# Attention features and FFN on one core: q and k transposed by VectorE in blocks of 32, v loaded in the matching token order

## The chip, the cores and the metric

One core of a Trainium2 chip runs the whole program. The metric is the device time of one execution in microseconds; several runs are made and their median is compared. Beside the timed runs there is one profiled execution, from which all durations of single instructions come.

## The reference

Polysketch attention, followed by a feed-forward network with a squared ReLU. All inputs and the output are fp32. There are 4 batches, 4 heads, 1088 tokens and a head width of 32; the FFN has width 128 and inner width 2048.

```python
def phi(x):                                   # features: 8 x 8 = 64 per token and head
    a = np.einsum('rd,bhsd->bhsr', S1, x)
    b = np.einsum('rd,bhsd->bhsr', S2, x)
    return np.einsum('bhsi,bhsj->bhsij', a, b).reshape(*x.shape[:-1], r * r)
q_p, k_p = (phi(q), phi(k))
kv = np.einsum('bhsf,bhsd->bhfd', k_p, v)     # summed over all tokens of a batch
z = np.sum(k_p, axis=2)
num = np.einsum('bhsf,bhfd->bhsd', q_p, kv)
den = np.einsum('bhsf,bhf->bhs', q_p, z)[..., None] + 1e-06
attn = (num / den)                            # then heads side by side: x is [4352, 128]
h = np.maximum(x @ w_in, 0.0)
out = h * h @ w_out
```

## The kernel before

**Tokens.** Of the 1088 tokens of a batch, 1024 are "main" tokens, eight consecutive ones on each of 128 partitions (token 8p + j on partition p). They are treated in two groups g of four, j = 4g to 4g + 3, so a group has 512 tokens: 4 tiles of 128 tokens. The last 64 tokens of each batch, the remainder, are treated by pairs of batches. A group of 512 tokens is a chunk for the FFN; with the remainder of all batches there are nine chunks, the eighth main one last.

**Features.** `load` fetches a batch of q, k or v as one transfer of 512 KB into a tile of the pool "inp" (two buffers for each of q, k and v). `proj_t` turns a group: for each head TensorE transposes 128x128 (partition p against j and head dimension) into PSUM (`xt_ps`, L194), and ScalarE copies it to `xt` (L59, the line of the helper `evict`; four buffers). `proj` multiplies `xt` with `w_bd`, a block-diagonal matrix of S1 and S2 (L180, `ab_ps`), ScalarE copies that out (`ab`), and POOL, in the start VectorE, makes the outer products (L221, `ph`). For k, `Kv` sums `ph` against v and a column of ones (L249, `kv_ps`), and VectorE copies the result to `kvbd`. For q, `feature_t` transposes `ph` by TensorE (L299, `t_ps`), `numerators` multiplies with `kvbd` (L180, `nd`), `normalize` divides on VectorE (L329 to L358, `xs`) and turns the quotient by TensorE (L370), which is `xT`, a chunk's input for the FFN.

**v.** The tile of `load` has 32 columns per head and token; `spread_v` copies it, one copy per head on POOL, to `v_main`, where each head has 33 columns, the last one of ones. `v_main` exists twice, for even and odd batches. `spread_vrem` does the same for the remainder. In the start, batch 0, ScalarE and POOL share the copies.

**FFN.** A chunk takes 16 blocks. In a block TensorE makes a `pg` (fp16, L534), ScalarE its ReLU (`gt`, L537), VectorE the square (`g2`, which the profile calls g, L538), and TensorE adds the product with `w_o` (fp32, L554, for the last chunk L563) to `po`. `first_product` runs two blocks ahead (`LOOK`). A finished chunk is copied and transposed back (L493, L497), scaled by VectorE (L511, `o_sb`, two buffers) and stored by SP (L519).

**Order.** `start()` is laid down by hand: batch 0's k, and q of its first group, down to the first `xT`; the second group's q is begun there (`second`). After it a scheduler orders the instructions of each engine; some, marked `pinned`, keep the program's order. The main loop runs over batches: two stretches of 16 blocks, between which `pump` emits steps of the waiting generators (`k_gen` of the next batch and `q_gen` of this one in the first stretch, `q_gen` of the next batch in the second). `drain` empties them. After the first stretch of batch b the loads of batch b + 2 are issued. All loads but four small ones and all stores are issued by SP, in one queue; each issue waits on one of eight semaphores, so that a transfer starts only when the one eight places before it has landed.

Of the kernel before, what the change touches and what calls it, by code (L numbers as in the profile page):

```python
# [8 lines left out]
F32 = mybir.dt.float32  # L9
# [12 lines left out]
def kernel(  # L22
# [39 lines left out]
    def pinned(ins):  # L62

        tc.keep_in_program_order(ins)
# [18 lines left out]
    def load(src, b, tag, pin=False):  # L83
        t = inpool.tile([128, H * NJ * D], F32, tag=tag)
        ins = load_part(t, src, b, 0, NJ)
        if pin:
            pinned(ins)
        return t

    def load_rem(src, r, eng, tag):  # L90
        t = inpool.tile([128, E], F32, tag=tag)
        for u in range(2):
            eng.dma_start(
                _v(t, 0, [[D, H], [1, D]], 64 * u, 64), rows(src, 2 * r + u, SM, 64, 1, 1)
            )
        return t

    s_nat = cpool.tile([16, E], F32)
    for i, src in enumerate((S1, S2)):
# [1 line left out]
            _v(s_nat, 0, [[D, H], [1, D]], 8 * i, 8),  # L101
            bass.AP(src.tensor, src.offset, [[D, 8], [0, H], [1, D]]),
        )
    k_sb, q_sb, v_sb, k_rm, q_rm, v_rm = {}, {}, {}, {}, {}, {}
    for x, tag in ((k_sb, "k_sb"), (q_sb, "q_sb"), (v_sb, "v_sb")):
        x[0] = inpool.tile([128, H * NJ * D], F32, name=f"{tag}0", tag=tag)
    load_part(k_sb[0], k, 0, 0, 4)
# [2 lines left out]
    load_part(q_sb[0], q, 0, 0, 4)  # L110
    load_part(v_sb[0], v, 0, 0, 4)
    load_part(v_sb[0], v, 0, 4, 4)
    v_rm[0] = load_rem(v, 0, nc.sync, "v_rm")
    w_in32 = cpool.tile([128, DFF], F32)
    for c in range(2):
        nc.sync.dma_start(
# [6 lines left out]
        bass.AP(moe_w_out.tensor, moe_w_out.offset, [[E, 128], [128 * E, NC], [1, E]]),  # L123
    )
    k_sb[1] = load(k, 1, "k_sb")
    v_sb[1] = load(v, 1, "v_sb")
    q_rm[0] = load_rem(q, 0, nc.sync, "q_rm")
    q_sb[1] = load(q, 1, "q_sb")


# [7 lines left out]
    w_bd = cpool.tile([128, H * 16], F32)  # L138
    nc.vector.memset(w_bd[:], 0.0)
    kvbd = [cpool.tile([128, 4 * VW], F32, name=f"kvbd{i}") for i in range(2)]  # L140
    v_main = [cpool.tile([128, NJ * H * VW], F32, name=f"v_main{i}") for i in range(2)]
    v_rem = [cpool.tile([128, H * VW], F32, name=f"v_rem{i}") for i in range(2)]
    iden16 = cpool.tile([128, 128], F16)
    nc.vector.tensor_copy(iden16[:], iden[:])
    for i in range(2):
        nc.vector.memset(kvbd[i][:], 0.0)
        nc.vector.memset(_v(v_rem[i], D, [[VW, H]]), 1.0)
        nc.vector.memset(_v(v_main[i], D, [[VW, H * NJ]]), 1.0)

    def idle_products(n):  # L150
        idle_ps = pspool.tile([128, 512], F32, name="idle_ps", tag="po", bufs=2)
# [6 lines left out]
    def spread_v(b, eng, j0=0, w=NJ, heads=range(H), pin=False):  # L158

        for h in heads:  # L160
# [4 lines left out]
            )  # L165
            if pin:
                pinned(ins)

    def spread_vrem(r, eng, pin=False):
        ins = eng.tensor_copy(  # L170
            out=_v(v_rem[r], 0, [[VW, H], [1, D]]), in_=_v(v_rm[r], 0, [[D, H], [1, D]])
        )
        if pin:
            pinned(ins)

    def tiled(out_ps, c0, w, lhsT, l0, rhs, n=128, p0=0, m=32):

# [9 lines left out]
    def proj_t(src, g, T, eng, tag="ms"):  # L187


        n = 4 if T == 4 else 1  # L190
        w = NJ * D if T == 4 else E
        xt_ps = pspool.tile([128, 512], F32, tag=tag, bufs=2)
        for i in range(n):
            nc.tensor.transpose(  # L194
                xt_ps[:, 128 * i : 128 * i + 128],
                src[:, w * i + 128 * g : w * i + 128 * g + 128],
                iden[:, :],
            )
        xt = apool.tile([128, 512], F32, tag="xt", bufs=4)
        evict(eng, xt[:, 0 : 128 * n], xt_ps[:, 0 : 128 * n])  # L200
        return xt

    def proj(xt, T, tag, eng, outer, ps_tag="ms", m=32):
# [68 lines left out]

    def k_gen(b, outer):
        eng = nc.scalar
        spread_v(b, nc.gpsimd, pin=True)
        if b % 2 == 0:
            spread_vrem(b // 2, nc.gpsimd, True)
        xt = []
        for g in range(2):
            xt.append(proj_t(k_sb[b], g, 4, eng))  # L280
            yield 1
        phs = []
        for g in range(2):
            phs.append(proj(xt[g], 4, "ph_k", eng, outer))
            yield 2
        if b % 2 == 0:
            yield from krem_gen(b // 2, eng, outer)
        kv = Kv(b)
        for g in range(2):
            kv.tiles(phs[g], g, range(4))  # L290
            yield 1
        kv.finish((nc.vector, nc.vector))
        yield 1
# [80 lines left out]
        return beta  # L374

    chunks = []

    def chunk_of(b, g, xT, beta):
        dst = bass.AP(out.tensor, out.offset + (b * S + 4 * g) * E, [[NJ * E, 128], [1, 512]])
        chunks.append((xT, 4, [(beta, 4)], [(dst, 0, 128, 0, 512)]))  # L380

    def x_gen(b, g, phT, m=32):
        nd = numerators(b, phT, m)
# [5 lines left out]

    def q_gen(b, g, outer, m=32):  # L390
        eng = nc.scalar
        xt = proj_t(q_sb[b], g, 4, eng)
        yield 1
        ph = proj(xt, 4, "ph_q", eng, outer, m=m)
        yield 3
        phT = []
        for pr in range(2):
            phT.append(feature_t(ph, 4, pr, eng))
            yield 1
        yield from x_gen(b, g, phT)  # L400
# [105 lines left out]
    def store(po, betas, dsts):  # L506

        o_sb = fpool.tile([128, 512], F32, tag="o_sb", bufs=2)
        t0 = 0
        for beta, n in betas:  # L510
            nc.vector.tensor_tensor(  # L511
                out=_v(o_sb, 128 * t0, [[128, n], [1, 128]]),
                in0=_v(po, 128 * t0, [[128, n], [1, 128]]),
                in1=_v(beta, 0, [[1, n], [0, 128]]),
                op=mult,
            )
            t0 += n
        for dst, p0, n, c0, w in dsts:
            nc.sync.dma_start(dst, _v(o_sb, c0, [[1, w]], p0, n))  # L519

    LOOK = 2
    LAST = 8
# [63 lines left out]
    def start():  # L586
        s_ps = pspool.tile([128, 16], F32, name="s_ps", tag="po", bufs=2)
        xk = [proj_t(k_sb[0], 0, 4, act)]
        nc.tensor.transpose(s_ps[:, :], s_nat[:, :], iden[0:16, 0:16])
        for h in range(H):  # L590
            nc.vector.tensor_copy(
                out=_v(w_bd, 16 * h, [[1, 16]], 32 * h, 32),
                in_=_v(s_ps, 0, [[1, 16]], 32 * h, 32),
            )
        xk.append(proj_t(k_sb[0], 1, 4, act))
        idle_products(2)
        pk = [proj(x, 4, "ph_k", act, (dve,), "pg", m=64) for x in xk]
        idle_products(1)
        xq = proj_t(q_sb[0], 0, 4, act)
        spread_v(0, act, 0, 4)  # L600
        pq = proj(xq, 4, "ph_q", act, (dve,), "pg", m=64)
        xkr = proj_t(k_rm[0], 0, 1, act)
        spread_v(0, act, 4, 4, (0, 1))
        spread_v(0, pool, 4, 4, (2, 3))
        spread_vrem(0, pool)
        ph_krem[0] = proj(xkr, 1, "ph_kr", act, (dve,), "pg", m=64)
        kv0 = Kv(0, 64, "po", 2)
        kv0.tiles(pk[0], 0, range(4))
        pqT = [feature_t(pq, 4, 0, act)]
        kv0.tiles(pk[1], 1, range(4))  # L610
        pqT.append(feature_t(pq, 4, 1, act))
        kv0.finish((dve, dve))
        first = x_gen(0, 0, pqT, 64)
        next(first)
        for c in range(4):
            act.copy(
                w_in[:, 512 * c : 512 * c + 512], w_in32[:, 512 * c : 512 * c + 512]
            )
# [13 lines left out]
    for b in range(B):  # L632
        add_work(second if b == 0 else q_gen(b, 1, (pool,)))
        if b + 1 < B:
            add_work(k_gen(b + 1, (pool,)))
        if b % 2 == 0:
            add_work(qrem_phi_gen(b // 2, (pool,)), qrem_num_gen(b))
        else:
            add_work(qrem_num_gen(b))
        for c in range(NC):  # L640
            block()
            pump_stores()
            pump(2)
        drain()
        if b + 2 < B:
            k_sb[b + 2] = load(k, b + 2, "k_sb", True)
            v_sb[b + 2] = load(v, b + 2, "v_sb", True)
            q_sb[b + 2] = load(q, b + 2, "q_sb", True)
            if b == 0:
                k_rm[1] = load_rem(k, 1, nc.sync, "k_rm")  # L650
                v_rm[1] = load_rem(v, 1, nc.sync, "v_rm")
                q_rm[1] = load_rem(q, 1, nc.sync, "q_rm")
        if b + 1 < B:
            add_work(q_gen(b + 1, 0, (pool,)))
        for c in range(NC):
            block()
            pump_stores()
            pump(2)
        if b + 1 < B:
            drain()  # L660
# [35 lines left out]
```

## Time and profile before

| | |
|---|---|
| three runs | 219.83, 217.87, 219.4 us; median 219.4 us |
| profiled execution | 217.62 us, span 215.8 us, mean granted TensorE clock 0.997 |
| TensorE matmuls (PE) | 207.4 us busy, 96% |
| VectorE (DVE) | 144.3 us, 67% |
| ScalarE (ACT) | 119.1 us, 55% |
| GpSimd (POOL) | 44.8 us, 21% |
| DMA | 11.35 MB, 13575 packets; above 3 tenths of the 16 DMA engines in 7 of 40 slices: the first five and two near 75 us |

The span is the time from the first to the last instruction of the profiled execution; 1.8 us of its time lie outside. PE is TensorE's matmuls, PEld its weight loads, which run beside matmuls. Matmuls are pipelined: a row's mean duration is longer than the distance between two of them. An fp32 matmul that is no transpose stands as two in the rows (a `po` is "x2"). An idle time is put down to what ended it.

### The profile page before, as it was taken

The page shows a single profiled execution, that of the slowest core. Times are in us where ns is not written, and L with a number is a line of the kernel's source. Part 1 is how long each engine was busy: PE and PEld are TensorE (multiplying, and loading weights), DVE is VectorE, ACT ScalarE, POOL GpSimd, SP SyncE. Part 2 cuts the span into 40 slices and gives each one's busy share as a digit, 9 for nine tenths or more (in the row PEclk, how much of TensorE's full clock was granted, in tenths as well). Part 3 has the DMA queues.
Part 4 walks back from the last instruction along what each step waited for, and adds up shares of the span by engine and source line. Part 5 has one row for each costly group of instructions (what it writes and reads, how often), then busy time and mean ns, then how long its engine had stood idle before and what let it go on. Part 6 is the DMA issues. An engine that isn't in the chain of part 4 may idle for free.

```text
span 215.8 us, 5391 instructions
## 1 busy us (share of the span) xinstructions
PE 207.4 (96%) x2253; PEld 125.4 (58%) x2253; DVE 144.3 (67%) x279; ACT 119.1 (55%) x234; POOL 44.8 (21%) x59
## 2 busy tenths in 40 slices
PE   8889999999999999999999999999999899999992
PEld 7677545445545664655546565455545454669992
DVE  2637696658685799557775567657868777677661
ACT  3655654564566555556466663656465456665550
POOL 1302273004050672004120960013101200000000
PEclk9999999999999999999999999999999999999998
DMA  6999900001000460001000100000000000100001
GB/s 172 270 312 319 267 8 3 2 3 49 3 0 0 131 212 3 3 0 52 2 0 0 52 3 2 3 16 36 2 3 19 30 5 0 49 0 15 12 0 49
DMA packets 13575, 11.35 MB, mean 53 GB/s; under 512 B 3824, under 2 KB 11760, under 8 KB 13552
## 3 DMA queue, kind: packets, MB, share of 16 engines
q1 hardware_dynamic: 12928, 10.95, 17.0%
q8 instruction: 17, 0.28, 0.5%
q10 hardware_dynamic: 624, 0.07, 0.2%
q14 instruction: 6, 0.05, 0.1%
HBM read 8.79 MB, written 2.23 MB: 51 GB/s over the span
## 4 chain that ended last, share of the span: by engine, by line
PE 86%; DVE 6%; ACT 1%; issue 1%; DVEq 0%
PE po L554 46%; PE pg L534 14%; PE po L563 7%; PE nd L180 5%; PE t_ps L299 4%; PE kv_ps L249 3%; PE xt_ps L194 3%; PE ab_ps L180 2%; PE o_ps L497 2%; DVE g L538 1%; DVE xs L358 1%; PE x_ps L370 1%; DVE o_sb L511 1%; DVE small L339 1%; ACT xt L59 1%
## 5 line engine op out<-in xcount | busy, mean ns | idle before, releaser
L538 DVE TENSOR_TENSOR g<-gt 128x512 f32<-128x512 f32 (+1 forms) x144 | 104.8, 737 | 50.5 <-ACT gt L537 48.5
L554 PE MATMUL po<-g,w_o 128*128 128x512 f32 (+1 forms) x256 | 124.1, 570 | 1.1 <-DVE g L538 1.1
L537 ACT ACTIVATE gt<-pg 128x512 f32<-128x512 f32 (+1 forms) x144 | 82.6, 576 | 48.2 <-PE pg L534 47.4
L554 PEld LDWEIGHTS po<-g,w_o 128*128 128x128 f32 x256 | 46.7, 191 | 27.8 <-DVE g L538 9.6
L534 PE MATMUL pg<-xT,w_in 128*128 128x512 f16 x128 | 48.6, 381 | 0.1
L221 POOL TENSOR_TENSOR ph<-ab 128x512 f32<-128x512 f32 (+1 forms) x27 | 32.1, 1213 | 69.7 <-ACT ab L59 69.6
L534 PEld LDWEIGHTS <-w_in 128*128 128x128 f16 x144 | 14.2, 99 | 17.7 <-issue 15.0
L59 ACT COPY sb<-t_ps 128x512 f32<-128x512 f32 (+1 forms) x20 | 10.3, 521 | 12.9 <-PE t_ps L299 12.9
L563 PEld LDWEIGHTS po<-w_o,g 128*128 128x128 f32 x128 | 16.3, 192 | 0.8 <-DVE g L538 0.4
L563 PE MATMUL po<-w_o,g 128*128 128x128 f32 x128 | 16.4, 275 | 0.0
L59 ACT COPY xt<-xt_ps 128x512 f32<-128x512 f32 (+1 forms) x20 | 10.3, 524 | 7.1 <-PE xt_ps L194 7.0
L364 POOL TENSOR_TENSOR beta<-mp 128x4 f32<-128x4 f32 (+1 forms) x10 | 3.1, 319 | 52.3 <-DVE mp L346 44.4
L59 ACT COPY ab<-ab_ps 128x256 f32<-128x256 f32 (+1 forms) x20 | 6.8, 340 | 13.0 <-PE ab_ps L180 12.5
L180 PEld LDWEIGHTS nd<-kvbd,sb 128*32 128x32 f32 (+1 forms) x512 | 8.9, 111 | 7.3 <-issue 3.2
L299 PEld LDWEIGHTS t_ps<-iden,ph 128*128 128x128 f32 x68 | 8.4, 141 | 8.0 <-issue 4.9
L180 PE MATMUL ab_ps<-w_bd,xt 128*32 128x64 f32 (+1 forms) x476 | 11.6, 223 | 1.1 <-ACT xt L59 1.1
L180 PEld LDWEIGHTS ab_ps<-w_bd,xt 128*32 128x32 f32 (+1 forms) x476 | 8.7, 113 | 6.5 <-ACT gt L537 3.0
L180 PE MATMUL nd<-kvbd,sb 128*32 128x66 f32 (+1 forms) x512 | 10.8, 222 | 0.7 <-DVE kvbd L60 0.7
L299 PE MATMUL t_ps<-iden,ph 128*128 128x128 f32 x68 | 10.9, 276 | 0.2 <-DVE ph L221 0.2
L194 PEld LDWEIGHTS xt_ps<-iden,t 128*128 128x128 f32 x52 | 6.4, 141 | 5.2 <-issue 2.8
L194 PE MATMUL xt_ps<-iden,t 128*128 128x128 f32 x52 | 8.3, 276 | 0.1
L249 PEld LDWEIGHTS kv_ps<-v_main,ph 128*32 128x32 f32 (+1 forms) x448 | 5.7, 113 | 2.7 <-issue 0.9
(57 smaller groups left out, 115.6 us busy)
## 6 DMA issues: line engine op xcount, KB each, us to landing
out_dram<-o_sb SPq DMA_DIRECT2D x8, 256.0 KB, 2.0
t<-in_k_dram SPq DMA_DIRECT2D x3, 512.0 KB, 6.5
t<-in_v_dram SPq DMA_DIRECT2D x3, 512.0 KB, 7.5
t<-in_q_dram SPq DMA_DIRECT2D x3, 512.0 KB, 7.3
w_in<-in_moe_w_in_dram SPq DMA_DIRECT2D x2, 512.0 KB, 6.0
k_sb<-in_k_dram SPq DMA_DIRECT2D x2, 256.0 KB, 3.1
q_sb<-in_q_dram SPq DMA_DIRECT2D x2, 256.0 KB, 5.7
v_sb<-in_v_dram SPq DMA_DIRECT2D x2, 256.0 KB, 5.6
```

Of the source, the lines that this page charges most:

```text
L59: return nc.scalar.copy(dst, src)
L180: nc.tensor.matmul(out_ps[p0 + c : p0 + c + m, c0 : c0 + w], lhsT[:, l0 + c : l0 + c + m], rhs,)
L194: nc.tensor.transpose(xt_ps[:, 128 * i : 128 * i + 128], src[:, w * i + 128 * g : w * i + 128 * g + 128], iden[:, :],)
L221: outer[(t0 // 2) % len(outer)].tensor_tensor(out=_v(ph, 256 * t0, [[64, 4 * m], [8, 8], [1, 8]]), in0=_v(ab, 64 * t0, [[16, 4 * m], [1, 8 ...
L249: nc.tensor.matmul(self.ps[c : c + self.m, VW * pr : VW * pr + VW], _v(ph, c0 + 128 * pr + c, [[1, self.m]], p0, n), _v(vt, v0 + VW * (2 * ...
L299: nc.tensor.transpose(t_ps[:, 128 * t : 128 * t + 128], ph[:, 256 * t + 128 * pr : 256 * t + 128 * pr + 128], iden[:, :],)
L497: nc.tensor.transpose(o_ps[:, 128 * t : 128 * t + 128], oT[:, 128 * t : 128 * t + 128], iden[:, :])
L534: nc.tensor.matmul(pg[:, 0:nt], w_in[:, 128 * c : 128 * c + 128], xT[:, 0:nt])
L537: nc.scalar.activation(gt[:, 0:nt], pg[:, 0:nt], Relu)
L538: nc.vector.tensor_tensor(out=g2[:, 0:nt], in0=gt[:, 0:nt], in1=gt[:, 0:nt], op=mult)
L554: nc.tensor.matmul(po[0][:, 0:nt], w_o[:, 128 * c : 128 * c + 128], g2[:, 0:nt], start=(c == 0), stop=(c == NC - 1),)
L563: nc.tensor.matmul(po[0][:, 128 * t : 128 * t + 128], g2[:, 128 * t : 128 * t + 128], w_o[:, 128 * c : 128 * c + 128], start=(c == 0 and t ...
```

## The change

Of the sixteen groups of main tokens of k and q, twelve are no longer transposed by TensorE: `turned` has VectorE transpose the whole 128x512 group at once, each block of 32x32 in itself, straight from the loaded tile to `xt`. Only batch 0's k, the first group of q of batch 0 and the last group of q of batch 3 (`BY_PE`) stay with TensorE. Since the blocks stay in their places, a tile of 128 tokens of a turned group holds other tokens than before: tile a has on partition 32j + p' the token 8(32a + p') + 4g + j. v and the output have to follow. `load_v` loads v of batches 1 to 3 straight into `v_main` in this order, by 32 transfers (2 groups, 4 heads, 4 values of j), each to 32 partitions with four runs of 128 bytes on each; the copies of POOL for these batches go. The remainder of v is loaded straight into `v_rem`. A chunk of a turned group is stored by four transfers of 32 partitions instead of one. In the start q_rm[0] is loaded ahead of v of batch 1, and the constant columns of `v_main` and `v_rem` are written before the first loads.

```diff
+    def load_v(b, pin=False):
+        for g in range(2):
+            for h in range(H):
+                for j in range(4):
+                    ins = nc.sync.dma_start(
+                        _v(
+                            v_main[b % 2], 4 * VW * 4 * g + VW * h,
+                            [[4 * VW, 4], [1, D]], 32 * j, 32,
+                        ),
+                        bass.AP(
+                            v.tensor,
+                            v.offset + ((b * H + h) * S + 4 * g + j) * D,
+                            [[NJ * D, 32], [32 * NJ * D, 4], [1, D]],
+                        ),
+                    )
+                    if pin:
+                        pinned(ins)
...
     k_sb[1] = load(k, 1, "k_sb")
-    v_sb[1] = load(v, 1, "v_sb")
     q_rm[0] = load_rem(q, 0, nc.sync, "q_rm")
+    load_v(1)
     q_sb[1] = load(q, 1, "q_sb")
...
+    def turned(src, g):
+        xt = apool.tile([128, 512], F32, tag="xt", bufs=4)
+        nc.vector.transpose(out=xt[:, :], in_=_v(src, 128 * g, [[NJ * D, 4], [1, 128]]))
+        return xt
...
     def k_gen(b, outer):
         eng = nc.scalar
-        spread_v(b, nc.gpsimd, pin=True)
-        if b % 2 == 0:
-            spread_vrem(b // 2, nc.gpsimd, True)
         xt = []
         for g in range(2):
-            xt.append(proj_t(k_sb[b], g, 4, eng))
+            xt.append(turned(k_sb[b], g))
             yield 1
...
+    BY_PE = ((0, 0), (B - 1, 1))
...
+            dsts = [
+                (
+                    bass.AP(
+                        out.tensor, at + j * E, [[NJ * E, 32], [32 * NJ * E, 4], [1, E]]
+                    ),
+                    32 * j, 32, 0, 512,
+                )
+                for j in range(4)
+            ]
...
-        xt = proj_t(q_sb[b], g, 4, eng)
+        xt = proj_t(q_sb[b], g, 4, eng) if (b, g) in BY_PE else turned(q_sb[b], g)
...
             k_sb[b + 2] = load(k, b + 2, "k_sb", True)
-            v_sb[b + 2] = load(v, b + 2, "v_sb", True)
+            load_v(b + 2, True)
             q_sb[b + 2] = load(q, b + 2, "q_sb", True)
             if b == 0:
                 k_rm[1] = load_rem(k, 1, nc.sync, "k_rm")
-                v_rm[1] = load_rem(v, 1, nc.sync, "v_rm")
+                load_rem(v, 1, nc.sync, "v_rm", v_rem[1], VW)
                 q_rm[1] = load_rem(q, 1, nc.sync, "q_rm")
```

More of the change, by code (lines that the diff above doesn't have):

```diff
@@ L88, in load, with load_rem @@
         return t
-    def load_rem(src, r, eng, tag):
-        t = inpool.tile([128, E], F32, tag=tag)
+    def load_rem(src, r, eng, tag, t=None, w=D):
+        if t is None:
+            t = inpool.tile([128, E], F32, tag=tag)
         for u in range(2):
             eng.dma_start(
-                _v(t, 0, [[D, H], [1, D]], 64 * u, 64), rows(src, 2 * r + u, SM, 64, 1, 1)
+                _v(t, 0, [[w, H], [1, D]], 64 * u, 64), rows(src, 2 * r + u, SM, 64, 1, 1)
             )
         return t
+    def load_v(b, pin=False):
[15 more added lines that the diff above has]
+                        pinned(ins)
     s_nat = cpool.tile([16, E], F32)
@@ L103 @@
         )
-    k_sb, q_sb, v_sb, k_rm, q_rm, v_rm = {}, {}, {}, {}, {}, {}
+    k_sb, q_sb, v_sb, k_rm, q_rm = {}, {}, {}, {}, {}
+    v_main = [cpool.tile([128, NJ * H * VW], F32, name=f"v_main{i}") for i in range(2)]
+    v_rem = [cpool.tile([128, H * VW], F32, name=f"v_rem{i}") for i in range(2)]
+    for i in range(2):
+        nc.vector.memset(_v(v_rem[i], D, [[VW, H]]), 1.0)
+        nc.vector.memset(_v(v_main[i], D, [[VW, H * NJ]]), 1.0)
     for x, tag in ((k_sb, "k_sb"), (q_sb, "q_sb"), (v_sb, "v_sb")):
@@ L112 @@
     load_part(v_sb[0], v, 0, 4, 4)
-    v_rm[0] = load_rem(v, 0, nc.sync, "v_rm")
+    load_rem(v, 0, nc.sync, "v_rm", v_rem[0], VW)
     w_in32 = cpool.tile([128, DFF], F32)
@@ L140 @@
     kvbd = [cpool.tile([128, 4 * VW], F32, name=f"kvbd{i}") for i in range(2)]
-    v_main = [cpool.tile([128, NJ * H * VW], F32, name=f"v_main{i}") for i in range(2)]
-    v_rem = [cpool.tile([128, H * VW], F32, name=f"v_rem{i}") for i in range(2)]
     iden16 = cpool.tile([128, 128], F16)
@@ L146 @@
         nc.vector.memset(kvbd[i][:], 0.0)
-        nc.vector.memset(_v(v_rem[i], D, [[VW, H]]), 1.0)
-        nc.vector.memset(_v(v_main[i], D, [[VW, H * NJ]]), 1.0)
     def idle_products(n):
@@ L167, in spread_v @@
                 pinned(ins)
[L169 to L174, printed above, removed]
     def tiled(out_ps, c0, w, lhsT, l0, rhs, n=128, p0=0, m=32):
@@ L376 @@
     chunks = []
+    BY_PE = ((0, 0), (B - 1, 1))
     def chunk_of(b, g, xT, beta):
-        dst = bass.AP(out.tensor, out.offset + (b * S + 4 * g) * E, [[NJ * E, 128], [1, 512]])
-        chunks.append((xT, 4, [(beta, 4)], [(dst, 0, 128, 0, 512)]))
+        at = out.offset + (b * S + 4 * g) * E
+        if (b, g) in BY_PE:
+            dsts = [(bass.AP(out.tensor, at, [[NJ * E, 128], [1, 512]]), 0, 128, 0, 512)]
+        else:
+            dsts = [
[7 more added lines that the diff above has]
+            ]
+        chunks.append((xT, 4, [(beta, 4)], dsts))
     def x_gen(b, g, phT, m=32):
@@ L518, in store @@
         for dst, p0, n, c0, w in dsts:
-            nc.sync.dma_start(dst, _v(o_sb, c0, [[1, w]], p0, n))
+            nc.sync.dma_start(dst, _v(o_sb, c0, [[E, w // E], [1, E]] if n == 32 else [[1, w]], p0, n))
     LOOK = 2
@@ L604, in start @@
         spread_v(0, pool, 4, 4, (2, 3))
-        spread_vrem(0, pool)
         ph_krem[0] = proj(xkr, 1, "ph_kr", act, (dve,), "pg", m=64)
```

## The prediction

> **What bounds the kernel now.** I read the page's first rows, then the chain of waits, then the timelines of PE, VectorE and SP where the change touches them. The busy row and the chain say that TensorE sets the time:
>
> ```profile
> PE 207.4 (96%) x2253; PEld 125.4 (58%) x2253; DVE 144.3 (67%) x279; ACT 119.1 (55%) x234; POOL 44.8 (21%) x59
> ```
>
> ```profile
> 46.48 0.86 PE po L554 x2
> 47.34 0.44 PE xt_ps L194 x4
> 47.99 0.86 PE po L554 x2
> ...
> 72.58 0.45 PE xt_ps L194 x4
> 73.05 0.59 ACT xt L59
> 74.44 0.86 PE po L554 x2
> ```
>
> In the chain (start, length, what) one FFN block is 0.22 us of pg (L534) and 0.86 us of po (L554), 1.08 us; blocks follow each other without a hole, and every other matmul group is inserted between two blocks at its full length. Four transposes of q or k (L194) take 0.44 us. At 73.05 TensorE also waits 0.6 us for the copy of such a transpose by ScalarE; the same is at 120.10. VectorE and ScalarE have idle time on average.
>
> The loads go through one queue, SP:
>
> ```profile
> 8.71 4.46 SPq L79 DMA_DIRECT2D t<-in_k_dram  x1
> 13.22 0.86 SPq L79 DMA_DIRECT2D t<-in_v_dram  x1
> ...
> 16.76 0.60 SPq L79 DMA_DIRECT2D t<-in_q_dram  x1
> 17.47 0.44 SPq L79 DMA_DIRECT2D t<-in_k_dram  x1
> ...
> 22.50 1.27 SPq L93 DMA_DIRECT2D t<-in_v_dram  x2
> ```
>
> Here a line is start, time on the queue, transfer. q of batch 1 is issued at 16.76 and k of batch 2 at 17.47. A transfer of 128-byte runs to half of the partitions (L93) costs 0.61 us of issue, and the pairs follow each other 1.32 us apart (22.50, 23.82), so 0.66 us each.
>
> **The change, part by part.** *Removed on TensorE:* 12 groups of 4 transposes, and 12 copies of 0.59 us on ScalarE, which is not the limit. One group, q(0,1) at 16.1, and the two of k of batch 1 (20.8 to 24.4) lie in the start, treated below. The other nine each cost the chain 0.44: 9 x 0.44 = 4.0 us (bounds 3.5 to 4.0). The two waits for ScalarE go too, 2 x 0.6 = 1.2. Gain 5.1 us.
>
> *Added on VectorE:* 12 transposes of 128x512 fp32. The trace has none. The nearest row is one pass over 128x512 fp32, 0.69 us, 0.61 from start to start; below it stands the cast of 128x128 at 0.23 (four of them would be 0.9, one launch for all some 0.45), above it the products that met GpSimd's, 1.16 to 1.22. I take 0.61. Beside a block of 1.08 us and its product g (L538, 0.69) one transpose fits with 0.2 us missing, and g is made about 0.75 us early. Four of them come at 82 to 87 us between the normalization's steps, where VectorE is busy 5.52 of 6 us: 4 x 0.61 less the lead and less the 1.5 us of kv matmuls that need no g there: I charge 0.5 us (0 to 1.5; 12 x 0.6 spread over such places if a transpose takes 1.2).
>
> *The start, 18 to 26 us.* The transpose of q(0,1) stands behind xs on VectorE, so its projection on TensorE starts at about 19.7, not 17.5, and x_ps, queued behind it and four idle products, at 21.4, not 19.1. The first g moves from 21.2 to 23.4. Between there and the nd of q(0,1) (25.91) TensorE loses two groups of transposes and its other transposes now run in the hole, so that nd starts at 25.9 again: 0 (-0.5 to +1). Two transposes of k of batch 1 stand there too; that load lands 10.1 us after 8.71, at 18.8, in time.
>
> *Moved: v.* POOL loses 12 copies (6.1 us) and one v_rem copy per pair of batches; POOL is idle 79% of the time, so 0. SP gets 32 transfers for one, each 16 KB in 128-byte runs on 32 partitions, three times. The first 32 stand in front of q of batch 1, and k of batch 2 stands behind it. VectorE's queue in the changed program is: the seventh g, two transposes of q of batch 1, the eighth g, a transpose of k of batch 2, the ninth g. Before, this place looks so:
>
> ```profile
> 30.98 0.69 DVE L358 TENSOR_TENSOR xs<-nd,small 128x512 f16<-128x512 f32 x1
> 31.59 3.42 DVE L538 TENSOR_TENSOR g<-gt 128x512 f32<-128x512 f32 x3
> ```
>
> ```profile
> 32.56 1.12 PE L554 MATMUL po<-g,w_o 128*128 128x512 f32 x2 [0.15 <-DVE g L538]
> 33.61 0.77 PE L249 MATMUL kv_ps<-v_main,ph 128*32 128x33 f32 x64
> 34.31 0.39 PE L534 MATMUL pg<-xT,w_in 128*128 128x512 f16 x1
> 34.54 1.02 PE L554 MATMUL po<-g,w_o 128*128 128x512 f32 x2
> ```
>
> The seventh g runs from 31.59, its po at 32.56, and the eighth po at 34.54. So VectorE comes to the transposes of q at 32.2. When does q land? A transfer waits until the eighth before it has landed (the queue's waits in the built program), so the sixth of the 32 starts no earlier than the landing of k of batch 1, 18.8. Then 27 spacings of s each, then q. After a quiet queue a 512 KB load landed 4.4 us after its issue (k at 72.29). So q lands at 18.8 + 27s + 4.4, and the eighth po can start 0.61 + 0.61 + 0.69 + 0.15 = 2.06 us later: it is late by 27s - 9.3 us against 34.54. The second half of kv waits for the last of the 32, inside the same hole; k of batch 2 lands while VectorE does q. Behind the waiting transpose stand all further g on VectorE; TensorE has one pg and the first half of kv and then waits for the eighth g, and ScalarE for free gt buffers: all of the lateness is paid.
>
> The price of s is the disputed one. From below: the small S1/S2 loads cost 0.28 (and 0.61), plain stores 0.33 to 0.36, plus 0.05: s = 0.33, no lateness. From above:
>
> ```profile
> L93 SPq DMA_DIRECT2D t<-in_v_dram x4: 613/616/722, 3.7 to 23.2; - x4
> L93 SPq DMA_DIRECT2D t<-in_q_dram x4: 614/744/1677, 14.1 to 24.5; - x4
> ```
>
> (min, median, max in ns.) None of the half-partition loads was under 0.61, whether 256 runs or, as stores of 64 rows, 64 runs (0.59). The new ones are nearest to these in run length and part of the partitions: s = 0.66. q is then issued at 36.6, lands at 41.0, the eighth po starts at 43.1: 8.5 us late (0 to 8.5).
>
> [...]
>
> A hole of 8 us also costs clock:
>
> ```profile
> 212.00:214.00 2.00, 0.00 (x0) 0.00 (x0) 0.67 (x1) 0.00 (x0) 0.00 (x0) 1.00 0.22 87
> 214.00:215.80 1.80, 0.00 (x0) 0.00 (x0) 0.00 (x0) 0.00 (x0) 0.00 (x0) 0.59 0.13 49
> ```
>
> In these windows (length, busy PE, PEld, DVE, ACT, POOL, granted clock) the last matmul ended at 211.9, and a mean of 0.59 over the last 1.8 us means half clock from 214.3: 2.4 us after. At the start the transposes of k took 1.11 us a group at 5.02, those of q 0.60 at 7.97: work has to run for 3 to 5 us at half speed first. Cost 1.5 to 2.5, taken as 2.0 (0 if the hole stays under 2.4).
>
> [...]
>
> *Later loads and stores.* 32 transfers take 21 us of SP after 37 and after 74 us. The first store, issued at 50.25 before, then goes out at about 63; its buffer is written again at 97. k of batch 3 is read from 84, lands about 79; q of batch 3 lands near 100 and is read at 121; v of batches 2 and 3 has 25 us or more. Six stores become four transfers each, 24 x 0.6 on a queue that idles 20 us before each store. All 0 behind these margins.
>
> **Sum.** Own time of the profiled execution 217.6 (span 215.8, 1.8 around it): - 5.1 + 8.5 + 2.0 + 0.5 = 223.5 us. The median of the runs, 219.4, lies 1.8 above the profiled one, so a median could be up to 225.
>
> **Rivals.** (1) *SP keeps up*, s up to 0.36: no wait, -5.1 + 0.5 = 213.0 us, faster. For it: the stores and the S load. Against: no row of this shape. It turns where the lateness and clock eat 4.6 us: s = 0.45 to 0.51. (2) *Half late*, s about 0.5, midway: 4.2 late, clock 0 to 2, 217.2 to 219.2: no change. (3) *VectorE becomes the bound*: no hole in the loads, but a transpose takes 1.2 us as beside GpSimd; nine of them, 0.6 more each, cost up to 5.4: about 218.4. Against: VectorE is 67% busy and g has a lead. That fewer transposes leave TensorE than said can be ruled out: 48 are missing in its queue.
>
> **Numbers.** Forecast 0.55; rival 1 0.25; rival 2 0.15; rival 3 0.05. About 1% (2.2 us) is what a measurement here tells from no change. Slower by over 1%: 0.55; within: 0.20; faster: 0.25. The forecast's own range is 220 to 227 (s from 0.55 up, clock and dense stretch at their bounds, median or profiled run); with rival 1 the whole is 213 to 227.
>
> **What would show it.** Right: L194 at 20 instructions instead of 68; the L105 transfers 0.6 us or more each; VectorE's transposes of t waiting for in_q_dram for over 5 us near 32 us; the granted clock under 1 just after; blocks at 1.08 us from there on. Wrong: transfers of 0.35 us, or q of batch 1 landing before 33 us, or transposes over 1 us.

## The result, and the profile after

The changed kernel takes 225.7 us (median of 4 runs, 224.3 to 227.0), the kernel before 218.6: ratio 1.035, 95% interval 1.030 to 1.041. It is slower. The profiled execution took 226.6 us, its span is 224.8 (before 217.6 and 215.8).

Runs of one kernel differ by 1 to 6 us, only in part with the granted clock (one of the kernels below: 220.6 us at 1.00, 222.2 at 0.991; another: 215.9 at 0.999, 218.8 at 0.996), so the medians here are of all runs, while the ratios compare the means of those within 1.5% of the kernel's fastest. The table of stretches sets single profiled executions side by side. In the diffs a line of three points stands for lines left out.

The busy row of the page (us, share of the span, instructions) says that TensorE's busy time hardly changed (48 matmuls fewer, but some at half clock, as shown below), and that its idle time (the span less the busy time) grew from 8.4 us to 16.5:

```profile
PE 208.3 (93%) x2205; PEld 123.6 (55%) x2205; DVE 148.2 (66%) x291; ACT 112.9 (50%) x222; POOL 36.7 (16%) x45
```

The chain of waits shows SP's queue for the first time. It leads from the landing of k of batch 1 through the v transfers to q of batch 1, from there to VectorE's transposes, and to the eighth po:

```profile
8.28 11.12 DMA t<-in_k_dram
19.41 0.02 issue
19.42 0.31 SPq L105
...
21.20 1.39 SPq L105
...
30.71 1.65 SPq L105
...
34.29 4.05 DMA t<-in_q_dram
38.35 0.02 issue
38.37 1.30 DVE xt L222 x2
39.68 0.58 DVE g L570
40.26 0.04 issue
40.30 2.07 PE po L586 x2
```

Between 19.42 and 34.29 lie exactly 27 transfers: 0.43 us each (the first 0.31) and 0.04 to the next one (all v transfers, ns, min/median/max: first row below), but for two of 1.39 and 1.65, so 0.55 on average. The second row is VectorE's new instruction, 0.70 us:

```profile
L105 SPq DMA_DIRECT2D v_main<-in_v_dram x96: 311/430/1737, 14.6 to 96.8; - x96
L222 DVE STREAM_TRANSPOSE xt<-t x11: 668/698/711, 19.4 to 129.0; 128x512 f32<-128x512 f32 x11
```

TensorE's timeline has three new holes (in brackets the idle time before, and what ended it): in the start, before the eighth po, and inside kv of batch 2:

```profile
19.52 1.12 PE L195 MATMUL ab_ps<-w_bd,xt 128*64 128x64 f32 x16 [2.71 <-DVE xt L222]
40.30 2.07 PE L586 MATMUL po<-g,w_o 128*128 128x512 f32 x2 [3.11 <-DVE g L570]
99.00 0.22 PE L271 MATMUL kv_ps<-v_main,ph 128*32 128x33 f32 x1 [1.53 <-issue]
```

Windows of 1 us (length, busy PE, PEld, DVE, ACT, POOL, granted clock, DMA) show half clock behind the first two. The clock is the third number from the end:

```profile
19.00:20.00 1.00, 0.48 (x9) 0.51 (x11) 0.94 (x2) 0.00 (x0) 0.00 (x0) 0.57 0.15 22
20.00:21.00 1.00, 1.00 (x15) 0.88 (x12) 0.73 (x2) 0.28 (x1) 0.00 (x0) 0.50 0.18 29
22.00:23.00 1.00, 1.00 (x11) 0.94 (x10) 0.42 (x1) 0.07 (x1) 0.00 (x0) 0.72 0.05 4
39.00:40.00 1.00, 0.00 (x0) 0.00 (x0) 1.00 (x3) 0.00 (x0) 0.00 (x0) 0.81 0.56 89
46.00:47.00 1.00, 1.00 (x20) 0.86 (x20) 0.45 (x2) 0.23 (x2) 0.00 (x0) 0.77 0.22 34
```

With 21 to 22 at 0.50 as well, the first stretch at half clock is 0.86 + 2 + 0.56 = 3.42 us; with 40 to 46 at 0.50, the second is 0.38 + 6 + 0.46 = 6.84 us, twice that.

To see where the time went, cut each profiled execution at the starts of the eight groups nd (TensorE's timeline; A is nd of q(0,0), B q(0,1), C that of the first remainder, E q(1,1), F q(2,0), G q(2,1), H q(3,0)). Lengths in us:

| kernel | A to B (start) | B to C (kv 1) | C to E | E to F (kv 2) | F to G | G to H (kv 3) |
|---|---|---|---|---|---|---|
| before | 10.79 | 14.52 | 39.65 | 23.22 | 24.09 | 23.28 |
| changed | 13.55 | 20.58 | 38.26 | 25.39 | 22.58 | 24.15 |
| q7_pinned | 12.20 | 14.52 | 38.44 | 24.92 | 22.68 | 24.29 |
| q8_pinned_q01 | 9.87 | 14.53 | 38.44 | 27.09 | 22.67 | 24.26 |
| q1_q_k_ahead | 12.40 | 16.25 | 38.26 | 25.33 | 22.58 | 24.17 |
| q2_q01_by_pe | 13.86 | 15.41 | 38.26 | 25.35 | 22.58 | 24.27 |
| q4_v_as_before | 13.63 | 15.70 | 38.29 | 26.71 | 22.61 | 22.84 |
| q14_q4_fill40 | 14.17 | 16.58 | 38.29 | 22.85 | 22.62 | 22.83 |
| q5_v_alone | 12.32 | 14.52 | 39.62 | 24.04 | 24.05 | 24.71 |
| q11_q8_fill40 | 9.87 | 15.15 | 38.45 | 23.54 | 22.67 | 25.58 |
| q13_before_fill96 | 10.77 | 14.52 | 39.65 | 23.22 | 24.09 | 27.08 |
| q10_pool_v | 10.11 | 14.93 | 38.50 | 26.79 | 22.74 | 22.92 |
| q12_q10_fill40 | 12.14 | 14.54 | 38.50 | 22.79 | 22.73 | 22.92 |
| q9_q_alone | 10.85 | 14.52 | 38.86 | 22.79 | 23.65 | 22.92 |

The changed kernel against before: +2.8 in the start, +6.1 with the hole, then gains of 1.4 and 1.5 as meant, and losses of 2.2 and 0.9 where kv of batches 2 and 3 lies; together 9.0 us, as much as the span grew. The experiments take these apart.

### The profile page after: what moved, and what is told of

Same layout as the page of the kernel before. It is cut to its first block, busy times and chain, and to the rows that moved or that the text cites. A ratio compares the mean times of both kernels' runs of the same rounds, so it can differ in the third digit from the quotient of the medians.

```text
span 224.8 us, 5449 instructions
## 1 busy us (share of the span) xinstructions
PE 208.3 (93%) x2205; PEld 123.6 (55%) x2205; DVE 148.2 (66%) x291; ACT 112.9 (50%) x222; POOL 36.7 (16%) x45
## 4 chain that ended last, share of the span: by engine, by line
PE 74%; DMA 9%; SPq 7%; DVE 6%; issue 2%; ACTq 1%; ACT 0%; DVEq 0%
PE po L586 42%; PE pg L566 12%; DMA t<-in_k_dram 7%; PE po L595 6%; SPq L105 6%; PE nd L195 3%; PE kv_ps L271 3%; DVE g L570 3%; PE t_ps L318 2%; PE ab_ps L195 2%; DMA t<-in_q_dram 2%; PE o_ps L529 1%; PE x_ps L389 1%; DVE o_sb L543 1%; DVE xt L222 1%
## 5 line engine op out<-in xcount | busy, mean ns | idle before, releaser
L570 DVE TENSOR_TENSOR g<-gt 128x512 f32<-128x512 f32 (+1 forms) x144 | 101.7, 714 | 48.2 <-ACT gt L569 45.4
L586 PE MATMUL po<-g,w_o 128*128 128x512 f32 (+1 forms) x256 | 126.1, 578 | 4.6 <-DVE g L570 4.6
L195 PE MATMUL ab_ps<-w_bd,xt 128*32 128x64 f32 (+1 forms) x476 | 12.1, 226 | 3.8 <-DVE xt L222 2.7
L392 ACT COPY xT<-x_ps 128x512 f16<-128x512 f16 x8 | 4.7, 586 | 14.0 <-PE x_ps L389 14.0
L271 PE MATMUL kv_ps<-v_main,ph 128*32 128x33 f32 (+1 forms) x448 | 9.0, 209 | 1.6 <-issue 1.5
L271 PEld LDWEIGHTS kv_ps<-v_main,ph 128*32 128x32 f32 (+1 forms) x448 | 7.7, 120 | 5.0 <-issue 2.8
L222 DVE STREAM_TRANSPOSE xt<-t 128x512 f32<-128x512 f32 x11 | 7.5, 694 | 3.4 <-DMA t<-in_q_dram 3.4
```

The lines of the kernel that those rows point to most:

```text
L195: nc.tensor.matmul(out_ps[p0 + c : p0 + c + m, c0 : c0 + w], lhsT[:, l0 + c : l0 + c + m], rhs,)
L222: nc.vector.transpose(out=xt[:, :], in_=_v(src, 128 * g, [[NJ * D, 4], [1, 128]]))
L271: nc.tensor.matmul(self.ps[c : c + self.m, VW * pr : VW * pr + VW], _v(ph, c0 + 128 * pr + c, [[1, self.m]], p0, n), _v(vt, v0 + VW * (2 * ...
L570: nc.vector.tensor_tensor(out=g2[:, 0:nt], in0=gt[:, 0:nt], in1=gt[:, 0:nt], op=mult)
L586: nc.tensor.matmul(po[0][:, 0:nt], w_o[:, 128 * c : 128 * c + 128], g2[:, 0:nt], start=(c == 0), stop=(c == NC - 1),)
```

## The experiments

The diffs are against the changed kernel, but for one that says otherwise. `pinned` keeps an instruction at its place in the program's text; without it the scheduler chooses.

**Where the waiting transposes stand.** q7_pinned:

```diff
-    def turned(src, g):
+    def turned(src, g, pin=True):
...
-        nc.vector.transpose(out=xt[:, :], in_=_v(src, 128 * g, [[NJ * D, 4], [1, 128]]))
+        ins = nc.vector.transpose(out=xt[:, :], in_=_v(src, 128 * g, [[NJ * D, 4], [1, 128]]))
+        if pin:
+            pinned(ins)
...
-        xt = proj_t(q_sb[b], g, 4, eng) if (b, g) in BY_PE else turned(q_sb[b], g)
+        xt = proj_t(q_sb[b], g, 4, eng) if (b, g) in BY_PE else turned(q_sb[b], g, (b, g) != (0, 1))
```

> Whole change, but VectorE's transposes keep the place in its queue that the program's text gives them (that of q(0,1) apart), so those of q of batch 1 stand near 48 us and not ahead of the eighth g. The loads are the same. Theory T: the wait near 35 us, the hole of TensorE and the second stretch at half clock are gone: -3.3 -2.0 -1; 219 to 220.5. Rival R (VectorE's added work is the bound wherever it stands): within 1 us of the changed kernel, 224.5 to 226.5.

Profiled 219.6 us, as expected; the median of the four runs, 223.0, is 2.5 us above the expectation (ratio 1.013, 1.003 to 1.023, from two of the four). What the other runs lost no trace shows; their clock was 0.984 and 0.985, that of the profiled one 0.995. In the profiled run B to C is 14.52 as before, to the hundredth: the whole hole of 6.1 us is gone, with the same late loads, and no VectorE row waits for in_q_dram. The 12 transposes are still there and no run comes to 224, so rival R falls. The start's 2.71 us of idle time are there too, and cost no half clock this time: A to B is 12.20, so about half of the changed kernel's 2.8 us there goes with the clock.

**The start.** q8_pinned_q01 adds one group to those of TensorE:

```diff
-    BY_PE = ((0, 0), (B - 1, 1))
+    BY_PE = ((0, 0), (0, 1), (B - 1, 1))
```

> As the pinned one, and q(0,1) is transposed by TensorE as before the change (with its stores in plain order). Theory T: the start's loss (2.4 us by the trace of the changed kernel, with its clock window at half speed) goes too: 217 to 218. Rival (the start's loss is that of the transposes of k of batch 1 on VectorE): as the pinned one, 219 to 220.5. Rival R: 224 to 226.

A to B is 9.87: 2.33 less than pinned, and 0.92 under before (the two groups of k of batch 1 are worth 2 x 0.44). The loss of the start is q(0,1) behind xs on VectorE. The median of 219.2 (ratio 1.003, 0.998 to 1.007) is above the 217 to 218 expected, and the table says where: E to F is 27.09, 3.9 more than before.

**The loads' order.** q1_q_k_ahead leaves VectorE's order to the scheduler:

```diff
     q_rm[0] = load_rem(q, 0, nc.sync, "q_rm")
-    load_v(1)
     q_sb[1] = load(q, 1, "q_sb")
...
     second = start()
+    k_sb[2] = load(k, 2, "k_sb")
+    load_v(1)
...
-            k_sb[b + 2] = load(k, b + 2, "k_sb", True)
+            if b > 0:
+                k_sb[b + 2] = load(k, b + 2, "k_sb", True)
```

> Whole change, VectorE's order left to the scheduler; only the loads are reordered: q of batch 1 and k of batch 2 are issued before the 32 transfers of v of batch 1. Theory T (the hole before the eighth g is nothing but the late landing of q behind those transfers): q lands before 30 us, no wait for in_q_dram, the 6 us that the stretch from nd of q(0,1) to nd of the remainder lost come down to 1 or less; the start, the dense stretch and kv of batches 2 and 3 stay; 225.7 - 5 = about 220.5. Rival R (VectorE is the bound there): 224 to 226.

Profiled 220.6 as expected, median 222.7, 2 us above it (ratio 1.023, 1.017 to 1.029). No wait for in_q_dram is left, and B to C falls by 4.3 us. The other 1.7 stay: now that its data is there, VectorE runs two transposes ahead of xs in this stretch (at 31.5 and 34.3), and kv starts late:

```profile
35.64 1.35 PE L270 MATMUL kv_ps<-v_main,ph 128*32 128x33 f32 x64 [1.08 <-POOL ph L242]
```

The row names GpSimd's ph, which runs at the same time in the pinned kernel (31.77 and 31.72) and for which no matmul waits there. TensorE's weight queue stands here from 33.65 to 35.58 in one wait, for VectorE and a load; the sixteen v transfers of that group had landed by 28.53, and xs ended at 35.54. The kernel with v as before (below) has the same order on VectorE and no v transfers, and its row names xs:

```profile
37.90 0.76 PE L271 MATMUL kv_ps<-v_main,ph 128*32 128x33 f32 x64 [1.12 <-DVE xs L378]
```

Its B to C is 1.2 us over before; pinned, the stretch has neither. So of the 6.1 us 4.3 are the late q with its half clock, and 1.7 stay with the place of the transposes, of which 1.2 stand in a kernel without v's transfers too.

**The start alone.** q2_q01_by_pe has the edit of `BY_PE` without the pinning:

> Whole change, loads as in it; only q(0,1) is transposed by TensorE, with its stores in plain order. Theory T (q of batch 1 lands at a fixed time, set by SP's queue): what the start gains is waited for again at the eighth g, so the time is the changed kernel's, 224.5 to 226.5, with a longer wait for in_q_dram. Rival (start and hole add up): 222.5 to 223.5.

Median 222.0 (ratio 1.019, 1.014 to 1.024): both expectations missed, the second by little but for the wrong reason. The start gained nothing (13.86), since the scheduler now put the transposes of k of batch 1 ahead of xs, and TensorE waited 2.94 us for xs. But the waiting transposes came to stand one g later:

```profile
37.86 1.31 DVE L222 STREAM_TRANSPOSE xt<-t 128x512 f32<-128x512 f32 x2 [1.31 <-DMA t<-in_q_dram]
```

q lands as late as in the changed kernel, VectorE waits 1.31 us and not 3.37, no clock is lost behind it (the half clock of this run is in the start), and B to C is 5.2 us shorter. The theory had taken VectorE's order for fixed.

**v as before.** q4_v_as_before:

```diff
+    v_sb[1] = load(v, 1, "v_sb")
     q_rm[0] = load_rem(q, 0, nc.sync, "q_rm")
-    load_v(1)
...
+        spread_v(b, nc.gpsimd, pin=True)
         xt = []
...
-            load_v(b + 2, True)
+            v_sb[b + 2] = load(v, b + 2, "v_sb", True)
```

> Left out: the turned token order of v (v is loaded by one transfer a batch and spread by GpSimd in natural order, as before the change), so kv pairs other tokens; the amount of work is the kernel's. All transposes of the change stay on VectorE. Theory T (the v transfers delay q of batch 1; the hole, the clock lost behind it and the waits before kv are all theirs; only the late transpose of q(0,1) in the start, +2.4 us, and the dense stretch, +1, are VectorE's): no wait of VectorE for in_q_dram near 38 us, blocks at full clock from 26 us on, kv groups of 1.5 us; 218.6 - 5.2 + 2.4 + 1 = about 217. Rival R (VectorE has become the bound, the late q only shows it): within 1.5 us of the changed kernel, 224 to 227.

Median 221.7 (ratio 1.014, 1.006 to 1.022), not 217: a miss by 4.7. The wait for q and the waits before kv are gone (G to H 22.84), but E to F is 26.71, 3.5 over before, in a kernel without the v transfers. TensorE stops there for 1.93 us at kv of batch 2 with "issue" as the reason, that is, for nothing that the profile shows:

```profile
94.60 0.25 PE L271 MATMUL kv_ps<-v_rem,ph 64*32 64x33 f32 x4 [1.93 <-issue]
```

So it does in the changed kernel (1.53), the pinned ones (1.06 and 1.71), q1 (1.32) and q2 (1.36); in the kernel before it does not.

**v alone.** q5_v_alone has all transposes on TensorE and the stores of before, and `load_v` reads v in natural order:

```diff
-                            v.offset + ((b * H + h) * S + 4 * g + j) * D,
-                            [[NJ * D, 32], [32 * NJ * D, 4], [1, D]],
+                            v.offset + ((b * H + h) * S + 4 * g + 256 * j) * D,
+                            [[NJ * D, 32], [D, 4], [1, D]],
...
-            xt.append(turned(k_sb[b], g))
+            xt.append(proj_t(k_sb[b], g, 4, eng))
...
-        xt = proj_t(q_sb[b], g, 4, eng) if (b, g) in BY_PE else turned(q_sb[b], g)
+        xt = proj_t(q_sb[b], g, 4, eng)
```

> The v part alone: all transposes stay on TensorE, stores as before, v of batches 1 to 3 by 32 transfers each into its blocks in natural order (runs of 512 bytes instead of four runs of 128 in DRAM; as many transfers and as many bytes). Theory T: q of batch 1 still lands near 38 us, but TensorE needs it only at about 47 us, so no hole; the kv groups wait for eight landings each: +0.8 us three times, and up to 1.5 more at kv(2); 221 to 222.5. Rival (the loads cost nothing where q comes in time): 218 to 219. Rival R: 218 to 219 too, since VectorE has no transposes here.

Median 219.1 (ratio 1.005, 1.002 to 1.008), 2 us under the expectation and just over the rivals' 218 to 219. No hole, as expected (B to C 14.52). kv of batch 2 costs 0.8 us more, of batch 3 1.4. The semaphore rows of kv on TensorE's weight queue, before and changed, name the reason: one wait for each of the transfers instead of one for the copy:

```profile
L249 PEldq EVENT_SEMAPHORE  x3: 51/51/51, 12.8 to 133.0; - x3
```

```profile
L271 PEldq EVENT_SEMAPHORE  x48: 51/51/1479, 12.6 to 142.7; - x48
```

A wait that is met at once takes 51 ns, but in the trace of q5_v_alone two that follow each other start 0.11 us apart. Ten of the sixteen fall inside kv of batch 2 and fourteen inside that of batch 3, so each costs 0.08 to 0.1 us; in batch 1, where FFN blocks stand between the parts of kv, they cost nothing. There is no stop at kv of batch 2. The start of this profiled run is 1.5 us longer than before, with a stop of 1.31 us by "issue" in a projection at 18.67.

**The stop.** Beside it lies a packet of the queue that the page calls "q8 instruction", 17 packets of 16 KB in all (before and changed). Between two of them the kernel before runs 122 matmuls on average (53 to 189) and as many weight loads, so some 250 instructions. kv of one batch is 144 such pairs in 1.56 us. Theory F: 18 to 28 matmuls fewer ahead of kv of batch 2 (rows of the traces; 993 before) have moved such a packet, taken for a fetch of TensorE's instructions, from before this group to its beginning, and then the group runs out of instructions. That the packet is such a fetch, and that the instructions run out, is the author's reading; the runs show where the packets lie and where TensorE stops. In the changed kernel the packet lies at 96.58, 1.2 us behind the first matmul of kv of batch 2; before, it lies at 82.13, 3.9 us ahead of it. In the fourteen profiled executions TensorE has thirteen stops of over 0.25 us with the reason "issue", and before twelve of them such a packet starts 2.35 to 3.1 us ahead of the next matmul, the one in the start of q5_v_alone included (15.90). Three kernels add 40 empty matmuls in the first 4 us, where TensorE waits for its first load (landed at 3.65 us in the kernel before). In the rows an empty matmul stands as two, so that with two idle products less all later matmuls move by 76 rows:

```diff
+    for i in range(40):
+        c = 32 * (i % 4)
+        nc.tensor.matmul(empty_ps[c : c + 32, 0:33], zero[:, c : c + 32], zero[:, 0:33])
-    idle_products(6)
+    idle_products(4)
```

> The pinned kernel with q(0,1) on TensorE, and 40 empty matmuls of 32x33 in the first 4 us, where TensorE waits for the first load (two of the six idle products are left out for them). They compute nothing that is used; they move the places at which TensorE's instructions are fetched by 40 matmuls against the work. Theory F (the stop of 1.7 us inside kv of batch 2, with the half clock behind it, is a 16 KB instruction fetch that 56 missing matmul instructions have moved into this group): no idle time put down to issue at kv of batch 2, kv there 2.4 us or less instead of 4.2; 219.2 - 1.8 - 1.3 = about 216. Rival W (the stop is a wait for v's landings or for their semaphores): unchanged, 218.5 to 219.5.

Median 217.3 (ratio 0.998, 0.994 to 1.002) against 219.2 without the empty matmuls, 1.3 above the expectation; the intervals of the two ratios overlap, so here the stretch shows the effect and not the total. kv of batch 2 falls from 4.17 to 2.3 us and E to F by 3.6. Part of it is given back at two other places: stops of 0.42 us in kv of batch 1 (the one without a packet close ahead; its cause stays open) and of 1.03 in kv of batch 3, 2.35 us behind a packet.

> Left out: the turned token order of v, as in the kernel with v loaded and spread as before. That kernel, with 40 empty matmuls in the first 4 us. It took 221.7 where theory T gave 217; theory F puts the 1.9 us stop at the end of kv of batch 2 and the half clock behind it (1.3) down to a fetch: 218 to 219. Rival (VectorE's dense stretch after 82 us is what cost it): 221 to 222.

E to F is 22.85, 3.9 less, so the stop, with the half clock behind it, is what that kernel lost there. But kv of batch 1 gets a stop of 0.68 us, and the median of 220.1 (ratio 1.009, 1.005 to 1.013) lies between the two expectations. What is left of the miss stands in the first two columns: 3.4 us in the start, where 2.4 were expected, and the transposes' place before C.

The reverse, an edit of the kernel before, with 96 empty matmuls and two idle products:

> The kernel before, unchanged but for 96 empty matmuls of 32x33 in the first 4 us (four of the six idle products are left out for them). Theory F: before, the fetch of 16 KB starts some 28 matmuls ahead of kv of batch 2 and lands in time; 96 more matmuls bring the next place of a fetch to the start of that group: a stop of 1 to 2 us there put down to issue, and perhaps half a clock window; 219.5 to 221.5. Rival W (TensorE's instructions come in time wherever they are cut): as before, 217.5 to 218.5.

Median 222.1, ratio 1.019 (1.015 to 1.023): 4.3 us slower by matmuls that cost nothing where they stand (A is at 15.08, before 15.05). The place was not the expected one. kv of batch 2 is untouched, and the stop is at the end of kv of batch 3, with half clock behind it (po 1.92 us instead of 1.02):

```profile
134.29 0.32 PE L253 MATMUL kv_ps<-v_rem,ph 64*32 64x33 f32 x14
136.81 0.27 PE L253 MATMUL kv_ps<-v_rem,ph 64*32 64x33 f32 x2 [2.20 <-issue]
```

The packet ahead of this stop lies at 134.2, the next matmul 2.6 us later. So far theory F holds: empty matmuls that nothing uses bring the stop into kv of one batch (2.20 us here) or take it out of another's (4.17 to 2.3 us above). What TensorE lacks in a stop no view shows. At which group it would come was not foreseen.

**A version that beats both.** q10_pool_v is the pinned kernel with q(0,1) on TensorE, and v loaded by one transfer a batch and moved into the matching order by GpSimd; q12_q10_fill40 adds the 40 empty matmuls:

```diff
+        for t in range(4):
+            for j in range(4):
+                pinned(
+                    nc.gpsimd.tensor_copy(
+                        out=_v(v_main[b % 2], 4 * VW * t, [[16 * VW, 2], [VW, H], [1, D]], 32 * j, 32),
+                        in_=_v(v_sb[b], D * j, [[4 * D, 2], [NJ * D, H], [1, D]], 32 * t, 32),
+                    )
+                )
...
-            load_v(b + 2, True)
+            v_sb[b + 2] = load(v, b + 2, "v_sb", True)
```

> As the one with 40 empty matmuls, but v of each batch is loaded by one transfer and brought into the matching token order by 16 GpSimd copies of 32 partitions (from partitions 32t.. to 32j..) instead of 32 transfers. Theory T (kv then waits for few semaphores and SP's queue is free): kv of batches 2 and 3 back at 1.5 us, so 2 us under the one with 40 empty matmuls, 213.5 to 215. Rival G (GpSimd's 8 us of copies a batch slow VectorE's products beside them, or hold ph of the q group behind them): no gain over that kernel or up to 3 us slower.

Median 214.6 us, ratio 0.986 (0.984 to 0.989): faster than before by 1.4% and than the changed kernel by 11 us. kv of batch 2 is back at 1.56 us, and no stop is left:

```profile
87.76 1.30 PE L277 MATMUL kv_ps<-v_main,ph 128*32 128x33 f32 x128
88.99 0.33 PE L277 MATMUL kv_ps<-v_rem,ph 64*32 64x33 f32 x16
```

The 48 copies take 27.6 us of GpSimd, without a cost that a stretch shows. (The profiled execution, 217.5 us, has half clock for 10.24 us in its start; from C on it is undisturbed.)

> The fastest kernel so far (VectorE's transposes pinned, q(0,1) on TensorE, v by one transfer a batch and GpSimd copies) without the 40 empty matmuls. Theory F: 24 matmuls are missing ahead of kv of batch 2, against 28 in the kernel with v as before, which stopped there for 1.9 us; so it stops here too, 214.6 + 1.9 and up to 1.3 of clock: 216.5 to 218. Rival W (the empty matmuls don't matter where kv waits for no landings): 214 to 215.

Median 216.9 (ratio 0.997, 0.994 to 1.000): without the empty matmuls 2.2 us of the gain are gone, and the stop is there:

```profile
86.28 0.32 PE L273 MATMUL kv_ps<-v_rem,ph 64*32 64x33 f32 x12
88.73 0.28 PE L273 MATMUL kv_ps<-v_rem,ph 64*32 64x33 f32 x4 [2.14 <-issue]
```

**Half the change.** q9_q_alone turns only five groups of q on VectorE, pinned; all of k and v is as before:

```diff
-            xt.append(turned(k_sb[b], g))
+            xt.append(proj_t(k_sb[b], g, 4, eng))
...
-    BY_PE = ((0, 0), (B - 1, 1))
+    BY_PE = ((0, 0), (0, 1), (B - 1, 1))
```

> Half of the change: only five groups of q (both of batches 1 and 2, the first of batch 3) are transposed by VectorE, kept in the program's order; all groups of k and q(0,1) stay on TensorE, so v is loaded and spread as before the change. Theory T (a group taken from TensorE is worth 0.44 us anywhere in the blocks; the loss is of v's transfers, of the start and of what befalls kv): 218.1 - 5 x 0.44 - 0.6 = about 215.3, at most 217, faster than the kernel before. Rival R (VectorE's transposes cost what they save): 218 to 220.

Profiled 215.4 as expected, median 217.1, just over the "at most 217", ratio 0.994 (0.991 to 0.998): faster by 0.6%. Each stretch with one group of q fewer is 0.4 us shorter than before (E to F, F to G and G to H: 0.43, 0.44, 0.36).

## Why the prediction was right, and where it was not

The forecast, slower by the late q, came true, and by the path that it named: 225.7 against 223.5, within the range. The size was in part luck. In the profiled execution, for which the sum was made, it is 226.6, 3.1 above, with two errors against each other: up to C the sum charged 8.5 for lateness and 2.0 for clock, 10.5, and measured were 8.6 (48.92 against 40.36); from C on it counted -4.6, and measured was +0.4. With the measured lateness of 5.8 in place of 8.5 it would have given 220.8. Its signs came out smaller too: transfers of 0.43 us and not 0.6, a wait for q of 3.37 and not 5.

- *The queue.* Right: 27 spacings behind the landing of k of batch 1 (19.4, forecast 18.8), then q, 4.05 us to land (4.4). The transposes stand ahead of the eighth g, as read from the program.
- *The spacing s.* Too large: 0.55 on average, not 0.66. The rows of half-partition loads were the wrong neighbours. The plain spacing is 0.47; two long transfers, of 1.39 and 1.65 us, bring the average to 0.55. With 0.55 the prediction's own formula, 19.4 + 27 x 0.55 + 4.05 + 2.06, gives the eighth po at 40.36; it started at 40.30.
- *The clock.* From the eighth po (5.8 late) to C (8.6 late) 2.8 us are lost, the forecast said 2.0. Half clock lasted 6.84 us behind the hole of 3.1 us; the prediction counted on 3 to 5.
- *The start.* Forecast 0, measured +2.8 from A to B (nd of q(0,1) at 28.34, not 25.9), outside its bounds of -0.5 to +1. The idle time of 2.71 us was foreseen in the delay of 2.2, but not that it reaches nd of q(0,1), and not that 3.42 us of half clock would follow: the pinned kernel has the same idle time at full clock and loses 1.4. Part of it would have been waited for at the eighth g anyway, since the chain above sets q's landing without it.
- *Gain on TensorE.* 0.44 a group holds; the two waits for ScalarE, 1.2 us of the sum, were not there. From C on the stretches are shorter by 1.36, 0.37, 1.47 and 0.44 where kv does not interfere (the kernel with v as before and 40 empty matmuls), 3.6 together; forecast were 5.1 less 0.5 for the dense stretch. The chain was misread there, as shown below the list.
- *VectorE's dense stretch.* Charged 0.5, about right: it shows as one idle time of TensorE in C to E, 0.40 us in the changed kernel (second fence below) and 0.41 in the one with v as before and 40 empty matmuls. Nine groups at 0.44 are 4.0; less this 0.4 that is 3.6.
- *Later loads.* Charged 0, behind margins for the landing. The landings were in time. But kv has to wait for sixteen semaphores a batch where one was, 0.8 and 1.4 us by the kernel with v alone, and that was not costed.
- *Fewer instructions.* Not thought of: with 48 matmuls fewer in TensorE's queue the packets of "q8 instruction" lie at other places, one of them at 96.58 in kv of batch 2, and TensorE stops there for 1.53 us.

The chain does name ScalarE's copy at 73.05 as what TensorE waited for. But the timeline of the kernel before shows TensorE at work beside that copy, with 32 matmuls of a projection:

```profile
72.41 0.60 PE L194 MATMUL xt_ps<-iden,t 128*128 128x128 f32 x4
72.94 0.65 PE L180 MATMUL ab_ps<-w_bd,xt 128*32 128x64 f32 x32
73.05 0.59 ACT L59 COPY xt<-xt_ps 128x512 f32<-128x512 f32 x1 [0.66 <-PE xt_ps L194]
73.69 0.42 PE L180 MATMUL nd<-kvbd,sb 128*32 128x66 f32 x8
```

TensorE stood idle for 0.09 us there, and for 0.09 at 120.6, the other place; the projection remains after the change. A chain names one cause for each stretch of time, which does not mean that TensorE stood still in it: that is read from TensorE's own timeline. The wait of the dense stretch, in the changed kernel, is an idle time:

```profile
86.12 1.13 PE L586 MATMUL po<-g,w_o 128*128 128x512 f32 x2 [0.40 <-DVE g L570]
```

Rival 3 (VectorE the bound, a transpose at 1.2 us) is wrong, since a transpose takes 0.70 us. But VectorE's order has a share: where q comes in time, transposes ahead of xs cost 1.2 to 1.7 us in the stretch before C. That is the scheduler's order, since pinning removes it.

## What to carry to other kernels

Before work is moved to another engine's queue, ask what each moved instruction waits for and what stands behind it there: here one place in VectorE's order was worth 5.2 us, half clock included, with the same data landing at the same time. The load cut in 32 was paid three times: in issue (0.43 us a transfer), in what was queued behind it (q of batch 1 landed at 38.34 us, 22.34 before), and in the sixteen waits of its reader (0.8 and 1.4 us). And when a dense group of small matmuls gets slower without any wait that the profile names, look at the packets of the instruction queue before you explain it by the edit: here one lay 2.35 to 2.8 us ahead of the end of ten such stops.

## What the runs showed of the hardware

- On the queue that the page calls "q8 instruction" a packet of 16 KB came per 122 pairs of weight load and matmul, on average, in the kernel before. In ten kv groups (144 pairs, in 1.56 us if nothing stops them) TensorE stopped for 0.7 to 2.2 us with such a packet 0.7 to 1.6 us behind the group's first matmul; the next matmul came 2.35 to 2.8 us after the packet. In the profile this is an idle time with the reason "issue". A packet near the end of a group stopped nothing (93.58 in q14_q4_fill40, 0.2 us before the end).
- Half clock came in stretches of 3.42 and 6.84 us, once of 10.24. In the changed kernel they began 2.3 and 2.4 us into the idle times of 2.71 and 3.11 us. The same idle time of 2.71 us in the start cost one stretch of 3.42 us there and none in the pinned kernel; no run shows why.
- A transfer of 16 KB to 32 partitions in runs of 128 bytes took 0.43 us of SP's queue, less than the 0.61 of the half-partition loads, with single ones up to 1.74.
- A transpose of 128x512 fp32 in blocks of 32 took 0.70 us on VectorE, as an elementwise pass over the same tile (0.69).
